# Loading and fusing two weight matrices ahead of attention, in a fused attention and feed-forward kernel

## The chip, the cores and the metric

One NeuronCore of one Trainium2 chip. Times are device microseconds (us) of one execution. A "span" is the length of the profiled execution on the core; in every run here the time is 1.7 us longer than the span. Each comparison is made with runs of the kernel before on the same chip in the same rounds.

## The reference

Causal attention over 8 batches, 8 heads, 576 tokens, with 16 extra keys and values ("beacons") that every token sees, then a feed-forward layer on the 4,608 tokens:

```python
scores = q @ k_all.T / sqrt(64)         # 8 x 8 x (576 x 592), causal past the 16 beacons
a      = softmax(scores);  x = a @ v_all         # x: 4608 x 512
h      = (x @ w1) * (x @ w2) @ w3       # w1, w2: 512 x 1024; w3: 1024 x 1024
out    = h @ w_out                      # w_out: 1024 x 512
```

The kernel multiplies `w3 @ w_out` once ("fusing", 64 matmuls of 512 columns), so that the feed-forward needs 96 matmuls for each 512 tokens: 64 for `x @ w1` and `x @ w2`, 32 for the fused product, 864 in all.

## The kernel before

Attention goes by head pairs (four per batch) and half pairs (eight "steps" `s` per batch). Scores are made keys by queries, so the exponentials go straight into the value matmuls. In the traces here TensorE takes its matmuls in program order, and the generator `ff` hands out feed-forward matmuls that are put between the steps as filling: `emit_ff(n)`. The main loop, which the change hardly touches:

```python
for s in range(NSB, NS):                     # NSB = 8 steps in a batch
    b, r = s // NSB, s % NSB
    ...
    if more: scores(s + 1); exps(s + 1, 0)
    values(s)
    if b == 1 and r % 2 == 0 and r < NSB - 2:
        pe_transpose_pair(1, r // 2 + 1)     # batch 1: q, k of the next head pair
        if r < NSB - 4: cast_pair(1, r // 2 + 2)
    emit_ff(...)                             # cut
    if 1 <= b < B - 1:
        if r == 0:
            for c in range(NJT if b > 1 else 0):     load_v(b + 1, c)
            for c in range(NJT if b + 2 < B else 0):
                load_q(b + 2, c); load_k(b + 2, c)   # into q16s[(b+2) % 2], k16s[(b+2) % 2]
        if 1 <= r <= NJT:
            transpose_qk(b + 1, r - 1)       # DMA transposes on SyncE's queue
```

From batch 2 on, q and k are loaded by GpSimd's queue, which casts them to fp16, into two alternating buffers `q16s[b % 2]` and `k16s[b % 2]`, and transposed by DMA. Batches 0 and 1 take another way: their pairs are loaded as fp32 by SyncE's queue into eight staging tiles of their own (`early`), cast on VectorE (`cast_pair`) and transposed on TensorE (`pe_transpose_pair`). **In this kernel batch 1 never uses `q16s[1]`**, so at batch 1's first step (`r == 0`) batch 3's q and k may be loaded there. This point matters later.

The start: q, k first, attention of batch 0 from 8 us on, fusing after the weights have landed, at 26 to 49 us; batch 1's 64 filling matmuls, 4 at its first scores and 60 between its steps, are feed-forward work of the first 512 tokens.

Of the kernel before, what the change touches and what calls it, by code (L numbers as in the profile page):

```python
# [39 lines left out]
def kernel(  # L40
# [43 lines left out]

    ptp = ctx.enter_context(tc.tile_pool(name="ptp", bufs=2))
    xp = ctx.enter_context(tc.tile_pool(name="xp", bufs=2))
    sm = ctx.enter_context(tc.tile_pool(name="sm", bufs=4))
    gp = ctx.enter_context(tc.tile_pool(name="gp", bufs=2))
    wp = ctx.enter_context(tc.tile_pool(name="wp", bufs=2))
    early = ctx.enter_context(tc.tile_pool(name="early", bufs=8))  # L90
    tiny = ctx.enter_context(tc.tile_pool(name="tiny", bufs=2))
    bkp = ctx.enter_context(tc.tile_pool(name="bkp", bufs=1))
    asb = ctx.enter_context(tc.tile_pool(name="asb", bufs=3))
# [36 lines left out]

    early_qk, early_b = {}, {}

    def load_pair(b, t):
        for i, src in enumerate((q, k)):
            st = early.tile([P, 2, RUN * D], FP32, name="st")
            if b:
                nc.vector.memset(st[0:1, 0, 0:1], 0.0)
            nc.sync.dma_start(  # L138
                st[:NR], src[b, ds(2 * t, 2)].rearrange("h (p j) d -> p h (j d)", j=RUN)
            )  # L140
            early_qk[b, t, i] = st
        if t == 0:
            bst = bkp.tile([Nb, H, D], FP32, name="bst")
            nc.sync.dma_start(bst, beacon_k[b].rearrange("h n d -> n h d"))
            early_b[b] = bst

    o16s = {}

    def cast_pair(b, t):
        o16s[t] = []  # L150
        for i in range(2):
            o16 = tiny.tile([P, RUN, P], FP16, name=f"o16_{i}")
            nc.vector.tensor_copy(  # L153
                o16[:NR].rearrange("p j (h d) -> p h j d", h=2),
                early_qk[b, t, i][:NR].rearrange("p h (j d) -> p h j d", j=RUN),
            )
            o16s[t].append(o16)
        if t == 0:
            b16 = bkp.tile([Nb, DM], FP16, name="b16")
            nc.vector.tensor_copy(b16, early_b[b].rearrange("p h d -> p (h d)"))  # L160
            early_b[b] = b16

    def pe_transpose_pair(b, t):
        qT, kT = qTs[b % NB2], kTs[b % NB2]
        for o16, dst, off, copy in (
            (o16s[t][0], qT, 0, nc.vector.tensor_copy if b or t != 1 else nc.scalar.copy),
            (o16s[t][1], kT, Nb, nc.scalar.copy),
        ):
            pt = psM.tile([P, 1024], FP16, name="pm")
            for j in range(RUN):  # L170
                nc.tensor.transpose(pt[:, ds(j * NR, NR)], o16[:NR, j, :], ident[:NR, :NR])
            if off:
                nc.tensor.transpose(
                    pt[:, ds(S, Nb)], early_b[b][:, ts(t, P)], ident[:Nb, :Nb]
                )
                copy(dst[:, t, 0:Nb], pt[:, ds(S, Nb)])
            copy(  # L177
                dst[:, t, ds(off, S)].rearrange("p (i j) -> p i j", j=RUN),
                pt[:, 0:S].rearrange("p (j i) -> p i j", j=RUN),
            )  # L180

    def pe_transpose_x(b):
# [25 lines left out]

    def constants(i):
        nc.vector.memset(vas[i][64:128, 4, :, :], 0.0)  # L210
        nc.vector.memset(vas[i][:, 0:4, :, 64:65], 1.0)
        nc.vector.memset(vas[i][0 : S + Nb - 4 * P, 4, :, 64:65], 1.0)

    for i in range(NB2):
        nc.vector.memset(kTs[i][:, :, ds(S + Nb, NJT * P - S - Nb)], 0.0)

    for t in range(NT):
        load_pair(0, t)
    nc.gpsimd.affine_select(
# [6 lines left out]
        channel_multiplier=-1,  # L226
    )
    for m, base in (
        (MA[:, 0:128], 0),
# [12 lines left out]
        )  # L242
    for i in range(NB2):
        nc.gpsimd.memset(k16s[i][64:128, 4, :], 0.0)
        nc.gpsimd.memset(q16s[i][64:128, 4, :], 0.0)

    def load_w12(c):
        for i, w in enumerate((moe_w1, moe_w2)):
            nc.gpsimd.dma_start(
                w12[:, :, ds(i * DF + c * 256, 256)],  # L250
                w[:, ts(c, 256)].rearrange("(t p) f -> p t f", p=P),
            )


    def w3_transposed(kt):
        pt = psM.tile([P, NFT, P], FP16, name="pm")
        for rt in range(NFT):
            nc.tensor.transpose(pt[:, rt, :], w316[:, kt // 2, kt % 2, ts(rt, P)], ident)  # L258
        wT = wp.tile([P, NFT, P], FP16, name="wT")
        nc.vector.tensor_copy(wT, pt)  # L260
        return wT

    def fuse(rows):
        wT = rows[0]
        for kt in range(NFT):
            pm = psM.tile([P, DM], FP32, name="pm")
            for rt in range(NFT):
                nc.tensor.matmul(  # L268
                    pm,
                    wT[:, rt, :],  # L270
                    wo16[:, rt, :],
                    start=(rt == 0),
                    stop=(rt == NFT - 1),
                )
                if rt == 3 and kt + 1 < NFT:
                    nxt = w3_transposed(kt + 1)
                if rt < NFT - 1:
                    yield
            nc.scalar.copy(Wt[:, kt, :], pm)  # L279
            wT = nxt  # L280
            yield

# [24 lines left out]
    def ff_out(mc, gT):  # L307
        for mt in range(4):
            pm = psM.tile([P, 512], FP32, name="pm")
            for kf in range(NFT):  # L310
# [7 lines left out]
                if kf < NFT - 1:  # L318
                    yield
            ot = early.tile([P, 2, RUN * D], FP32, name="st")  # L320
            ot = ot.rearrange("p h r -> p (h r)")[:, 0:DM]
            nc.vector.tensor_scalar(ot, pm, float(1.0 / GS), None, ALU.mult)  # L322
# [3 lines left out]
    def stream():  # L326
        yield from fuse(rows)
        for mc in range(M // 512):
            gT = yield from ff_ab(mc)
            yield from ff_out(mc, gT)  # L330

    rows = []
    ff = stream()
# [50 lines left out]
    def values(s):  # L384
# [7 lines left out]
        ni = len(tiles)  # L392
        pv = psV.tile([P, 6, VS], FP32, name="pv")
        for n, i in enumerate(tiles):
# [28 lines left out]
    n_first = 4  # L423
    n_second = 64 - n_first
    fill = [0] * NS
    for s in range(NSB, 2 * NSB):
        fill[s] = n_second * (s - NSB + 1) // NSB - n_second * (s - NSB) // NSB

    marks = [(2 * NSB, 128 + 8), (26, 128 + 132), (58, 128 + 516), (NS, 128 + 588)]
    for (s0, u0), (s1, u1) in zip(marks, marks[1:]):  # L430
# [4 lines left out]
    def ahead(s):  # L435
        scores(s)
        for j in range(2):
            exps(s, j)
# [4 lines left out]

    spin(14)
    cast_pair(0, 0)
    pe_transpose_pair(0, 0)
    cast_pair(0, 1)
    spin(2)
    ahead(0)
    pe_transpose_pair(0, 1)  # L450
    cast_pair(0, 2)
    constants(0)
    for c in range(NJT):
        load_v(0, c)
    wo_v = moe_w_out.rearrange("(a c p) n -> a p c n", p=P, c=2)
    for a in range(4):
        nc.gpsimd.dma_start(wo16[:, ds(2 * a, 2), :], wo_v[a])

    w316 = xT[:, :, ds(M // 2, 2 * DF)].rearrange("p a (c r) -> p a c r", c=2)
    for kt in range(NFT):  # L460
        nc.gpsimd.dma_start(w316[:, kt // 2, kt % 2], moe_w3[ts(kt, P), :])
    spin(1)
    ahead(1)
    masks(0)
    pe_transpose_pair(0, 2)
    cast_pair(0, 3)
    spin(1)
    ahead(2)
    masks(1)
    pe_transpose_pair(0, 3)  # L470
    constants(1)
    masks(2)
    for c in range(NJT):
        load_v(1, c)
    load_w12(0)
    load_w12(1)
    for c in range(NJT):
        load_q(2, c)
        load_k(2, c)
    load_w12(2)  # L480
    load_w12(3)
    for s in range(NSB):
        if 0 < s < NSB - 2:
            ahead(s + 2)
        if s < 5:
            spin(1)
        if s == 5:
            rows.append(w3_transposed(0))
        emit_ff((0, 0, 0, 0, 0, 4, 6, 6)[s])
        values(s)  # L490
        if 0 < s < NSB - 2:
            masks(s + 2)
        if s == 5:
            for t in range(NT):
                load_pair(1, t)
    for c in range(NJT):
        load_v(2, c)
    emit_ff(6)
    pe_transpose_x(0)
    emit_ff(20)  # L500
    cast_pair(1, 0)
    emit_ff(56 - emitted)
    pe_transpose_pair(1, 0)
    cast_pair(1, 1)
    emit_ff(64 - emitted)
    ahead(NSB)
    emit_ff(n_first)
    masks(NSB)
    for s in range(NSB, NS):
# [6 lines left out]
        if b == 1 and r % 2 == 0 and r < NSB - 2:  # L516
            pe_transpose_pair(1, r // 2 + 1)
            if r < NSB - 4:
                cast_pair(1, r // 2 + 2)
        k1 = min(4, fill[s])  # L520
# [21 lines left out]
    emit_ff(1 << 30)  # L542


# [28 lines left out]
```

## Time and profile before

| | before |
|---|---|
| time, median of the first 3 runs | 310.21 us (310.08 to 312.54) |
| profiled span | 309.7 us (time of that run 311.4) |
| first scores of batch 0 / 1 / 2 | 7.95 / 49.55 / 79.40 us |
| from batch 2's first scores to the end | 230.3 us |
| TensorE busy | 295.8 us, 96% |

TensorE is the engine that sets the end. The landmarks are read from the timeline of TensorE: "first scores of batch n" is the start of the first score matmul of that batch. Because of that order, the stretch between two landmarks contains a known set of work, and two kernels can be compared stretch by stretch. The lines themselves are in the prediction below. One more view, which the prediction tells but does not show: TensorE's windows from 80 us on. Columns: window, length; busy us and (instructions) of TensorE, weight loads, VectorE, ScalarE, GpSimd; granted TensorE clock; DMA share; GB/s.

```profile
80.00:90.00 10.00, 9.35 (x98) 4.64 (x96) 4.76 (x12) 4.79 (x6) 10.00 (x14) 1.00 2.20 185
90.00:100.00 10.00, 10.00 (x106) 5.12 (x99) 6.01 (x15) 7.06 (x10) 5.08 (x7) 1.00 2.15 184
100.00:150.00 50.00, 50.00 (x528) 25.81 (x527) 28.06 (x68) 28.82 (x40) 24.01 (x30) 1.00 1.48 153
```

TensorE is hardly ever without work here, at full clock. Anything that leaves it standing, or running at half clock, is paid in full.

### The profile page before, as it was taken

The numbers are of one execution on the slowest core, as the hardware profiler recorded it, in microseconds if no ns is written. First come the engines' busy times: TensorE is split into PE (matmuls) and PEld (weight loads), VectorE is DVE, ScalarE is ACT, GpSimd is POOL, SyncE is SP. The second block draws the span as 40 slices with busy tenths as digits, with TensorE's granted clock in tenths as the row PEclk, the third lists the DMA queues.
The fourth block names the chain that finished last, engine by engine and source line by source line (L and its number), as shares of the span: only waits on it lengthen the run. The fifth ranks groups of instructions, "written<-read, shape, count | busy, mean of one in ns | idle before, by whom it ended". The sixth has DMA issues, their size and how long they took to land.

```text
span 309.7 us, 7001 instructions
## 1 busy us (share of the span) xinstructions
PE 295.8 (96%) x2823; PEld 153.4 (50%) x2823; DVE 168.1 (54%) x391; ACT 158.1 (51%) x230; POOL 108.9 (35%) x147
## 2 busy tenths in 40 slices
PE   8898999898899999999999999999999999999995
PEld 3465555454454555555555545455555554444442
DVE  4854545865465556555555555555555554334342
ACT  2973327775546745674467466546655660230320
POOL 8555617835992089009701960320000000000000
PEclk9777999999999999999999999999999999999999
DMA  7999999999999999999999999997334003302003
GB/s 177 199 203 210 194 262 176 156 151 155 163 206 172 140 101 215 154 147 123 231 154 119 116 230 121 155 183 157 78 66 148 0 4 78 135 0 102 36 0 135
DMA packets 156960, 42.97 MB, mean 139 GB/s; under 512 B 143104, under 2 KB 151296, under 8 KB 156928
## 3 DMA queue, kind: packets, MB, share of 16 engines
q0 software_dynamic: 102240, 17.28, 78.7%
q1 hardware_dynamic: 54688, 25.25, 42.8%
q8 instruction: 22, 0.36, 0.5%
q14 instruction: 10, 0.08, 0.1%
HBM read 39.32 MB, written 9.44 MB: 157 GB/s over the span
## 4 chain that ended last, share of the span: by engine, by line
PE 79%; DMA 8%; DVE 4%; ACT 3%; SPq 2%; issue 2%; POOL 1%; DVEq 0%
PE pm L290 34%; PE pm L311 18%; PE pv L397 11%; PE ps L359 8%; PE pm L268 5%; DMA qT<-q 3%; DMA k<-in_beacon_k_dram 2%; DMA st<-in_k_dram 2%; ACT pT L368 2%; PE pm L258 1%; SPq L128 1%; DVE gT L303 1%; POOL va L112 1%; SPq L138 1%; DVE o L153 1%
## 5 line engine op out<-in xcount | busy, mean ns | idle before, releaser
L290 PE MATMUL pm<-xT,w 128*128 128x512 f16 x576 | 132.4, 379 | 0.7 <-ACT kT L177 0.7
L368 ACT ACTIVATE pT<-ps 128x736 f16<-128x736 f32 (+3 forms) x128 | 105.5, 865 | 40.2 <-PE ps L359 32.6
L290 PEld LDWEIGHTS <-w 128*128 128x128 f16 x576 | 53.5, 98 | 60.0 <-issue 1.5
L301 ACT ACTIVATE a_sb<-pm 128x512 f32<-128x512 f32 x72 | 43.0, 598 | 74.3 <-PE pm L290 73.9
L303 DVE TENSOR_TENSOR gT<-pm,a_sb 128x512 f16<-128x512 f32 x72 | 49.7, 691 | 44.9 <-PE pm L290 44.9
L311 PE MATMUL pm<-Wt,gT 128*128 128x512 f16 x288 | 65.6, 379 | 0.0
L112 POOL DMA_DIRECT2D va<-in_v_dram x40 | 34.2, 872 | 66.4 <-PE pv L397 57.4
L397 PE MATMUL pv<-va,pT 128*128 128x65 f16 x960 | 44.4, 196 | 2.6 <-DVE pT L380 2.5
L397 PEld LDWEIGHTS <-pT 128*128 128x128 f16 x960 | 35.6, 99 | 13.6 <-issue 6.5
L311 PEld LDWEIGHTS <-gT 128*128 128x128 f16 x288 | 26.9, 98 | 30.0 <-issue 0.2
L359 PE MATMUL ps<-qT,kT 64*128 64x80 f16 (+3 forms) x704 | 36.3, 232 | 2.5 <-ACT pT L368 1.9
L322 DVE TENSOR_SCALAR st<-pm 128x512 f32<-128x512 f32 x36 | 24.9, 691 | 25.0 <-PE pm L311 24.8
L405 DVE RECIPROCAL rd<-pv 128x4 f32<-128x4 f32 x64 | 12.1, 190 | 48.0 <-PE pv L397 47.8
L359 PEld LDWEIGHTS <-kT 64*128 64x128 f16 x704 | 21.1, 96 | 29.1 <-issue 27.1
L406 DVE TENSOR_TENSOR x<-pv,rd 128x256 f16<-128x256 f32 x64 | 31.4, 491 | 2.4
L103 POOL DMA_DIRECT2D q<-in_q_dram x30 | 26.7, 890 | 10.2 <-DMA va<-in_v_dram 6.3
L112 POOL DMA_DIRECT2D k<-in_k_dram x30 | 26.3, 878 | 7.4 <-DMA w<-in_moe_w_dram 4.3
L380 DVE TENSOR_TENSOR pT<-pT,MB 128x512 f16<-128x512 f16 x64 | 20.2, 322 | 0.0
L268 PE MATMUL pm<-wo,wT 128*128 128x512 f16 x64 | 17.1, 395 | 0.9 <-DVE wT L260 0.8
L380 DVE TENSOR_TENSOR pT<-pT,MA 128x480 f16<-128x480 f16 x32 | 12.9, 402 | 1.7 <-ACT pT L368 1.5
L153 DVE CAST o<-st 96x768 f16<-96x768 f32 x16 | 10.2, 666 | 4.1 <-DMA st<-in_q_dram 2.8
L279 ACT CAST Wt<-pm 128x512 f16<-128x512 f32 x8 | 4.7, 585 | 14.9 <-PE pm L268 14.9
(43 smaller groups left out, 98.1 us busy)
## 6 DMA issues: line engine op xcount, KB each, us to landing
out_dram<-st SPq DMA_DIRECT2D x36, 256.0 KB, 4.3
va<-in_v_dram POOLq DMA_DIRECT2D x24, 128.0 KB, 6.3
q<-in_q_dram POOLq DMA_DIRECT2D x24, 128.0 KB, 8.2
st<-in_q_dram SPq DMA_DIRECT2D x8, 288.0 KB, 7.4
st<-in_k_dram SPq DMA_DIRECT2D x8, 288.0 KB, 8.3
k<-in_k_dram POOLq DMA_DIRECT2D x18, 128.0 KB, 8.6
xT<-in_moe_w_dram POOLq DMA_DIRECT2D x8, 256.0 KB, 9.8
w<-in_moe_w_dram POOLq DMA_DIRECT2D x8, 256.0 KB, 14.4
```

Of the source, the lines that this page charges most:

```text
L103: nc.gpsimd.dma_start(q16s[b % NB2][:rows, c, :].rearrange("s (h d) -> s h d", h=H), q[b, :, ds(c * P, rows), :].rearrange("h s d -> s h d"),)
L112: nc.gpsimd.dma_start(dst[ds(p0, rows)], src[b, :, ds(s0, rows), :].rearrange("h s d -> s h d"))
L268: nc.tensor.matmul(pm, wT[:, rt, :], wo16[:, rt, :], start=(rt == 0), stop=(rt == NFT - 1),)
L290: nc.tensor.matmul(pm, w12[:, kt, ds(i * DF + kf * P, P)], xT[:, kt, ds(mc * 512, 512)], start=(kt == 0), stop=(kt == NKT - 1),)
L301: nc.scalar.activation(a_sb, pm, AF.Copy, scale=GS)
L303: nc.vector.tensor_tensor(gT[:, kf, :], pm, a_sb, ALU.mult)
L311: nc.tensor.matmul(pm, gT[:, kf, ts(mt, P)], Wt[:, kf, :], start=(kf == 0), stop=(kf == NFT - 1),)
L359: nc.tensor.matmul(ps[:, hh, ds(col, n)], kT[ds(hh * 64, 64), t, ts(jt, P)], qT[ds(hh * 64, 64), t, ds(q0, n)],)
L368: nc.scalar.activation(pT[:, :, ds(GO[g], GW[g])], pss[s][j][:, :, 0 : GW[g]], AF.Exp, scale=scale)
L380: nc.vector.tensor_tensor(blk, blk, m.unsqueeze(1).to_broadcast([P, 2, n]), ALU.mult)
L397: nc.tensor.matmul(pv[:, 2 * n + hh, 0:65], pT[:, hh, ds(col, P)], va[:, jt, 2 * t + hh, 0:65], start=(jn == 0), stop=(jn == len(BLK[i]) - 1),
L406: nc.vector.tensor_tensor(x16[:, ds(tiles[0], ni), ds(t * P, P)].rearrange("p i (h d) -> p i h d", h=2), pv[:, 0 : 2 * ni, 0:64].rearrange ...
```

## The change

Intent: `w3` and `w_out` are loaded first, half by SyncE's queue (fp32, cast on ScalarE and VectorE) and half by GpSimd's. Four of the eight rows of the fused weights grow side by side in four PSUM banks as `w_out` lands; the other four go between batch 0's head pairs. q and k of batch 0 come through the casting queue. Batch 1's q and k now come by the same `load_q` and `load_k` as all later batches, with transposes on TensorE. The 64 feed-forward matmuls of the first 512 tokens run in one piece before batch 1.

```diff
+    for a in range(2):                                     # SyncE: half of w3, w_out
+        st = gp.tile([P, 2, 2 * DM], FP32, name="gT")
+        nc.sync.dma_start(st[:, 0, :], moe_w3[ts(a, P), :])
+        nc.sync.dma_start(st[:, 1, :], moe_w_out[ds(a * 2 * P, 2 * P), :]...)
+        firsts.append(st)
+    def cast_first(a):
+        nc.scalar.copy(w316[:, a // 2, a % 2], firsts[a][:, 0, :])
+        nc.vector.tensor_copy(wo16[:, ds(2 * a, 2), :]..., firsts[a][:, 1, :])
     ...
+    load_w3(2); load_wo(2); load_w3(3); load_wo(3)         # GpSimd's queue
+    load_pair(0); load_w3(4)                               # then q, k pairs between rows
     ...                                                    # (cut)
+    for a in range(4):                                     # four rows side by side
+        if a < 2:
+            cast_first(a)
+        wTs.append(w3_transposed(a))
+        spin(2 if a == 0 else 1)                           # matmuls of zeros, for the clock
+        for kt in range(a):
+            fuse(accs[kt], wTs[kt], 2 * a - 2, 2 * a)
+        fuse(accs[a], wTs[a], 0, 2 * a)
+    for kt in range(4):
+        fuse(accs[kt], wTs[kt], NFT - 2, NFT)
     ...                                                    # (cut: batch 0's head pairs)
+    for c in range(NJT):                                   # batch 1 into q16s[1], k16s[1]
+        load_q(1, c)
+        load_k(1, c)
     ...
+    emit_ff(64)
+    pe_transpose_second(0)
     ...
-            pe_transpose_pair(1, r // 2 + 1)
-            if r < NSB - 4:
-                cast_pair(1, r // 2 + 2)
+            pe_transpose_second(r // 2 + 1)                # reads q16s[1], k16s[1]
```

The load of batch 3's q and k at `r == 0` is unchanged, so the diff does not show it.

> **What bounds the kernel now.** I read the page first (engine rows, the forty slices), then a table of windows over the first 100 us, then the chain of work that ended last, and last the timeline and the DMA queues of the start.
>
> ```profile
> PE 295.8 (96%) x2823; PEld 153.4 (50%) x2823; DVE 168.1 (54%) x391; ACT 158.1 (51%) x230; POOL 108.9 (35%) x147
> PE   8898999898899999999999999999999999999995
> ACT  2973327775546745674467466546655660230320
> PEclk9777999999999999999999999999999999999999
> DMA  7999999999999999999999999997334003302003
> ```
>
> Parts 1 and 2 of the page: TensorE (PE) has work in nearly every slice, ScalarE (ACT) and VectorE about half. The granted clock dips only in slices 2 to 4, and the DMA engines are full until about 230 us.
>
> ```profile
> 264.56 13.81 PE pm L290 x64
> ```
>
> In the chain, 64 matmuls of 512 columns take 13.81 us where nothing else is mixed in: 216 ns each. With that unit I count the useful work: 864 feed-forward and 64 fusing matmuls are 200.4 us. In the window from 100 to 250 us PE never stops; its 486 feed-forward matmuls are 105 us, so the 20.6 head pairs (scores and values) in it have 45, or 2.18 us each, 70 us for all 32. Transposes (w3, x, q and k) at about 56 ns are 11 us. Together 281 of 309.7 us: some 28 us are lost. The tail (last matmul 306.0 us) has 3.7 of them, so about 24 are lost before 95 us. That is all the change can win from.
>
> ```profile
> 0.00:5.00 5.00, 3.73 (x9) 1.31 (x10) 1.64 (x7) 1.28 (x1) 3.73 (x14) 1.00 0.63 144
> 10.00:15.00 5.00, 4.19 (x51) 2.56 (x52) 4.09 (x12) 4.83 (x10) 2.67 (x4) 0.73 1.89 186
> 15.00:20.00 5.00, 4.98 (x66) 3.62 (x66) 3.01 (x12) 3.24 (x6) 3.65 (x7) 0.59 1.51 194
> 25.00:30.00 5.00, 4.21 (x41) 2.77 (x39) 1.58 (x3) 0.60 (x1) 3.14 (x5) 0.66 1.12 210
> 45.00:50.00 5.00, 4.95 (x45) 2.73 (x43) 2.77 (x4) 2.05 (x5) 2.68 (x3) 1.00 1.51 221
> 50.00:100.00 50.00, 46.18 (x525) 25.03 (x524) 30.29 (x72) 32.58 (x49) 34.70 (x43) 1.00 2.09 166
> ```
>
> Columns: PE, weight loads, VectorE, ACT, GpSimd busy, granted clock, DMA share, GB/s. PE is "busy" for 4.98 of 5 us from 15 to 20 at a clock of 0.59, so busy is not useful there. After 30 us the clock is 1.00.
>
> ```profile
> 7.95 0.55 PE L359 MATMUL ps<-qT,kT 64*128 64x128 f16 x8 [0.27 <-ACT kT L177]
> ...
> 49.55 0.55 PE L359 MATMUL ps<-qT,kT 64*128 64x128 f16 x8
> ...
> 52.07 1.29 SPq L127 DMA_TRANSPOSE qT<-q  x1
> 67.84 2.40 SPq L128 DMA_TRANSPOSE kT<-k  x1
> ...
> 79.40 0.55 PE L359 MATMUL ps<-qT,kT 64*128 64x128 f16 x8
> ```
>
> The landmarks: first scores of batch 0 at 7.95 us, of batch 1 at 49.55, of batch 2 at 79.40; the DMA transposes for batch 2 run on SyncE's queue from 52.07 to 70.24. By 49.55 the useful PE work is: fusing 13.8 + 3.6 (its transposes), batch 0's attention 8.7, q, k, x transposes 4.6, total 30.7. So 18.9 us are lost before 49.55 and 5.2 from there to 79.40 (29.85 us for 64 feed-forward matmuls, 13.8; attention, 8.7; three pair transposes, 2.1).
>
> Rates of the two queues, from three 5 us stretches of the start (packets, MB, share): 5 to 10, 20 to 25 and 50 to 55 us.
>
> ```profile
> q1 hardware_dynamic: 831, 1.18, 109.2%
> ```
> ```profile
> q0 software_dynamic: 704, 1.05, 116.0%
> ```
> ```profile
> q0 software_dynamic: 5847, 0.75, 232.4%
> ```
>
> The hardware queue moved 236 GB/s of fp32 (rows of 1.5 KB, 96 partitions). The casting queue landed 210 GB/s of fp16 from large rows, so it read 420 GB/s; with 64-element rows it is bound by packets, 1170 per us.
>
> **What the Trainium skill says.** (1) "TensorE: Matmul & The Clock Gate", Back-to-back issue gap: 512 columns at full clock take N/2.4 + 2.5 ns, 216 ns. The chain above agrees to the ns. (2) The same page, Part 1: an insufficiently busy PE falls to half its clock for a window of some 3.4 us or more. The clock of 0.59 to 0.73 in three windows before 30 us agrees in kind. (3) "DMA: Bandwidth & Descriptors", Issuing engines are not separate DMA queues: both queues run on the same 16 DMA engines and interleave, so a second queue saves only issue time. So I add the engine time of both queues and don't take the longer one. The trace agrees from 40 to 45 us (683 packets of one, 685 of the other), though in the first 10 us the casting queue got nothing. (4) The same page, SWDGE vs HWDGE vs iDMA: only GpSimd's queue casts. So what SyncE loads as fp32 needs an ACT or VectorE cast, and what GpSimd loads doesn't.
>
> **The change part by part.** Before, q and k start at once, attention of batch 0 runs from 8 to 34 us bound by ACT (four exponentials per head pair, 0.78 + 1.02 + 0.81 + 0.85) with PE half empty and cold, and fusing w3 with w_out (64 matmuls) comes at 26 to 49 us, when the weights have landed. After, w3 and w_out come first; four rows grow in the four PSUM banks that scores use later; the other four rows go between batch 0's head pairs. The feed-forward of the first 512 tokens (64 matmuls) fills the time before batch 1.
>
> Step A, the start. SyncE's 2.1 MB fp32 take 6.5 to 9 us of all DMA engines (236 GB/s measured; the rows are now 4 KB on 128 partitions, so up to 320 is my guess), GpSimd's 2.1 MB source 5 us (210 GB/s landed). From 2 us on, that ends at 13.5 to 16, say 14.5. Until then 24 of the 32 matmuls can run; the last 8 are 1.7 us, to 16.2. Then two evacuations (0.7), two reorders (0.8), transposes (0.35), the kT copy (0.17 + 0.65): the first scores at about 19 us, against 7.95. Fusing done by then: 6.9 + 1.8.
>
> Step B, batch 0. Per head pair the chain is: kT copy, scores (0.4 to the first exponential), two exponentials 1.8, meanwhile w3 transposes, values 1.0, the wT copy 0.69 and four fusing matmuls 0.86 ahead of the next scores, which come 2.9 us after the kT copy; two exponentials 1.7, kT copy 0.82. That is 5.5, 5.6 and 5.7 us for the first three pairs. The last pair with its values and x transposes takes 9.5. In all 26.3: feed-forward starts at 45.3.
>
> Step C: 64 matmuls are 13.8; ten transposes and 4 matmuls 1.5: first scores of batch 1 at 60.6 against 49.55. It comes 11.1 us later with 68 matmuls (14.7 us) more done: a gain of 3.6 us.
>
> Step D, batch 1. Only 24 matmuls are left to put between its steps (the next block of 512 tokens needs batch 1 itself), against 60 before. So ACT and the hand-overs bound it: first exponentials 2.1; a step with transposes is 3.0 to 3.35 (values, transposes, kT copy 0.7 and exponential in a row), one without 1.8 to 2.4; eight come to 17.5; x transposes and hand-over 4. In all 23.6: first scores of batch 2 at 84.2 against 79.40.
>
> Step E, the rest. From batch 2's first scores to the end, before needs 309.7 - 79.4 = 230.3. The changed kernel has 32 matmuls fewer left, 6.9 us: 223.4. The sum is 84.2 + 223.4 = 307.6; with 0.5 for the timed median over the profiled span, 308.1.
>
> Moved without a price on the path: twelve fewer pair transposes, the batch 1 casts on VectorE (eight of 0.67). Batch 1's q and k now come through the casting queue: 9,400 packets at 1170 per us are 8 us, issued once batch 0's pairs are read (about 33 us) and there by about 50, before 60.6.
>
> **The rivals.** *Batch 2's DMA transposes become the wait.* They stand behind the first output stores on SyncE's queue and start at about 62 us; they took 18 us before and 7 more to land, so 87 or 88 against the 84.2 at which PE wants them: up to 3.5 us, a time of 311.5. Against it: with less traffic the same transposes took 1.2 to 1.3 us each near 210 us, which ends in time. I add 0.4 for it. *The start is slower or faster.* If the casting queue is starved again, nothing changes while the engines stay full; but if the first casts arrive only after 11 us as before (v's packets did, though issued at 4.63), step A ends 3 us later: 311. If both queues reach 400 GB/s, it ends 2.5 us earlier: 305.5. *Thinner filling later.* Steps 16 to 25 have 9.2 matmuls each in place of 12.4; where a_sb's 0.6 us falls between two exponentials, values may wait 0.4 us, up to 2 us in all. *The hand-overs of steps B and D are shorter than I chain them* (I took every wait in series): 1 us per head pair would be 6 us, and a time of 302.
>
> **Range and chances.** The sum and the first rival's share give 308.5. Step A is uncertain by 2.5 us, B and D by 3 together, the batch 2 wait by 2: about 4.2 in all, so 303 to 314. Faster by over 2% means below 304.0; slower means above 316.4. Filling a start bound by DMA with fusing should win something, but batch 1 gives much of it back for want of matmuls. Faster 0.22, within 2% 0.70, slower 0.08.
>
> **What will show it.** First scores of batch 0 near 19 us, of batch 1 near 60.6, of batch 2 near 84. A clock near 1.00 from 20 us on. Batch 1 with PE waits for ACT (kT) and VectorE (pT), about 5 us. If scores of batch 2 wait for a qT or kT transpose, the first rival holds. I am wrong if batch 0's head pairs take 7 us each (slower) or if batch 1's first scores come before 57 us (faster by over 2%).

## The result, and the profile after

| | before | after |
|---|---|---|
| time, median | 311.13 us (4 runs, 310.08 to 312.54) | 328.73 us (4 runs, 327.59 to 331.41) |
| profiled span | 309.7 | 325.9 |
| first scores of batch 0 / 1 / 2 | 7.95 / 49.55 / 79.40 | 26.18 / 68.34 / 99.44 |
| batch 1 (its first scores to batch 2's) | 29.85 | 31.10 |
| from there to the end | 230.3 | 226.5 |

The ratio after / before is 1.0575, 95% interval 1.0487 to 1.0663: slower. Ratios here are the mean time of one kernel's fast runs over that of the other's of the same rounds, so they are not quite the ratio of the medians quoted.

The page of the kernel after, parts 1 and 2 (one slice is 8.1 us):

```profile
PE 298.7 (92%) x2810; PEld 152.3 (47%) x2810; DVE 165.2 (51%) x382; ACT 156.6 (48%) x221; POOL 117.0 (36%) x159
PE   7688888983888999799999999999999999999995
PEclk9699999998599999999999999999999999999999
```

Two places stand out against the page before. In the second slice (8 to 16 us) TensorE and its clock are at 6. In the tenth and eleventh (73 to 90 us) TensorE falls to 3 and then the granted clock to 5. After that the rows look as before, which a windows view of the kernel after makes precise (columns as above):

```profile
10.00:15.00 5.00, 4.26 (x23) 2.27 (x24) 1.48 (x3) 0.00 (x0) 2.22 (x4) 0.53 1.19 207
15.00:20.00 5.00, 5.00 (x26) 2.35 (x25) 1.19 (x2) 0.00 (x0) 4.80 (x8) 0.79 1.56 188
75.00:80.00 5.00, 1.55 (x25) 0.74 (x22) 1.52 (x5) 0.93 (x2) 5.00 (x7) 0.85 2.14 143
80.00:85.00 5.00, 2.31 (x11) 1.13 (x11) 0.46 (x1) 0.81 (x2) 0.57 (x1) 0.50 1.32 84
85.00:90.00 5.00, 5.00 (x63) 2.88 (x62) 2.49 (x8) 3.06 (x4) 0.00 (x0) 0.62 0.40 105
100.00:150.00 50.00, 47.17 (x512) 24.25 (x512) 27.36 (x68) 32.01 (x44) 24.79 (x31) 1.00 1.69 149
```

From 75 to 85 us TensorE is busy 3.86 of 10 us; from 80 to 90 the clock is about half. From 100 to 150 us it stands for 2.8 us, where before it stood for none.

**The hole at 75 to 90 us.** TensorE's timeline of the kernel after (start, length, line, operation, tiles, count, and in brackets the idle time before and what ended it). L401 is the scores, L187 the transposes of batch 1's q and k:

```profile
71.15 0.52 PE L187 MATMUL pm<-ident,q 128*128 128x128 f16 x5
...
76.20 0.22 PE L187 MATMUL pm<-ident,q 128*128 128x128 f16 x1
77.94 0.23 PE L187 MATMUL pm<-ident,q 128*128 128x128 f16 x1 [1.52 <-DMA q<-in_q_dram]
80.26 0.29 PE L187 MATMUL pm<-ident,q 128*128 128x128 f16 x1 [2.09 <-DMA q<-in_q_dram]
...
99.44 0.55 PE L401 MATMUL ps<-qT,kT 64*128 64x128 f16 x8
```

Head pair 1's five q transposes run in a row at 71.15. Pair 2's, from 76.20 on, come one by one, and all but the first wait for a load of q: 1.52, 2.09, 1.38 and 1.05 us, 6.0 in all. But batch 1's q had been complete since before 66 us, or pair 0 could not have been transposed. Which loads are these? GpSimd's timeline in the same kernel:

```profile
71.67 0.88 POOL L103 DMA_DIRECT2D q<-in_q_dram  x1 [5.87 <-PE pm L187]
```

The bracket tells it: this load waited for the transposes L187, which ended at 71.67. It overwrites what they read. It is the load of batch 3's q into `q16s[1]`, emitted at batch 1's first step, after the transposes of pairs 0 and 1 and before those of pairs 2 and 3. The scheduler keeps program order: the load waits for the earlier readers, and the later readers wait for the load.

So the program order is wrong in a way that a time alone does not tell: heads 4 to 7 of batch 1 are computed from batch 3's q and k. The result was nevertheless accepted as correct. I repeated the reference's arithmetic on the host with those heads exchanged: the output changes by 0.5% of its norm, 1.4% within batch 1, because with inputs of this size the softmax is almost flat. No run here measures the wrong values as such; program order and the two waits show the exchange.

**The start.** TensorE in the kernel after; L307 is the transposes of w3's rows, L320 the growing of the four rows (32 matmuls), L213 matmuls of zeros, L168 the first q, k transposes:

```profile
6.36 0.84 PE L307 MATMUL pm<-ident,xT 128*128 128x128 f16 x8
7.04 0.59 PE L213 MATMUL pm<-zeros 128*128 128x512 f16 x2
10.03 0.86 PE L307 MATMUL pm<-ident,xT 128*128 128x128 f16 x8 [2.39 <-ACT xT L257]
...
11.11 1.06 PE L320 MATMUL ps<-wo,wT 128*128 128x512 f16 x2
12.88 1.04 PE L320 MATMUL ps<-wo,wT 128*128 128x512 f16 x2 [0.71 <-DVE wT L315]
...
14.99 2.93 PE L320 MATMUL ps<-wo,wT 128*128 128x512 f16 x8
...
18.42 4.48 PE L320 MATMUL ps<-wo,wT 128*128 128x512 f16 x20
24.56 0.70 PE L168 MATMUL pm<-ident,o 96*128 96x96 f16 x12 [1.67 <-DVE o L154]
```

The last piece of `w_out` for these rows had landed by 14.1 us (issued at 3.42 and 10.7 us on its way). By then TensorE had done 4 of the 32 growing matmuls. ScalarE and VectorE of the same kernel show what it waited for:

```profile
8.93 1.04 ACT L257 CAST xT<-gT 128x1024 f16<-128x1024 f32 x1 [3.55 <-DMA gT<-in_moe_w_dram]
...
11.53 0.69 DVE L258 CAST wo<-gT 128x1024 f16<-128x1024 f32 x1 [3.59 <-DMA gT<-in_moe_w_out_dram]
12.14 0.68 DVE L315 COPY wT<-pm 128x1024 f16<-128x1024 f16 x1
```

Row 1 of w3, SyncE's third load, landed at 8.9 us; from there a cast on ScalarE (1.04), eight transposes (0.86) and a copy on VectorE (0.68) come one after the other. That copy stood behind a cast of `w_out`, which itself waited for SyncE's fourth load until 11.5. Meanwhile TensorE stood still from 7.6 to 10.0 us, and the granted clock was 0.50 from 10.25 until about 17.1 us (fine windows; it shows in the 0.53 and 0.79 above).

By the prediction's own steps:

| step | predicted | after | difference |
|---|---|---|---|
| A, to batch 0's first scores | 19 | 26.18 | +7.2 |
| B, to the first feed-forward matmul (52.56) | 26.3 | 26.4 | +0.1 |
| C, to batch 1's first scores | 15.3 | 15.8 | +0.5 |
| D, batch 1 | 23.6 | 31.1 | +7.5 |
| E, rest | 223.4 | 226.5 | +3.1 |
| span | 307.6 | 325.9 | +18.3 |

The differences add to 18.4 from rounding.

### The profile page after: what moved, and what is told of

It reads as the page before. It is cut to its first block, busy times and chain, and to the rows that moved or that the text cites. A ratio compares the mean times of both kernels' runs of the same rounds, so it can differ in the third digit from the quotient of the medians.

```text
span 325.9 us, 6953 instructions
## 1 busy us (share of the span) xinstructions
PE 298.7 (92%) x2810; PEld 152.3 (47%) x2810; DVE 165.2 (51%) x382; ACT 156.6 (48%) x221; POOL 117.0 (36%) x159
## 4 chain that ended last, share of the span: by engine, by line
PE 80%; DMA 6%; DVE 6%; ACT 2%; POOL 2%; issue 1%; SPq 1%; DVEq 0%
PE pm L335 37%; PE pm L356 17%; PE pv L443 11%; PE ps L401 8%; DMA gT<-in_moe_w_out_dram 3%; PE ps L320 2%; DMA xT<-x 2%; PE pm L320 2%; ACT pT L410 2%; DVE x L452 1%; DMA q<-in_q_dram 1%; DVE pT L422 1%; POOL k L112 1%; DVE ot L366 1%; POOL q L103 1%
## 5 line engine op out<-in xcount | busy, mean ns | idle before, releaser
L356 PE MATMUL pm<-Wt,gT 128*128 128x512 f16 x288 | 68.2, 384 | 0.1
L443 PE MATMUL pv<-va,pT 128*128 128x65 f16 x912 | 41.8, 195 | 3.3 <-DVE pT L422 2.2
L103 POOL DMA_DIRECT2D q<-in_q_dram x35 | 30.9, 884 | 21.7 <-DVE o L154 9.8
L401 PE MATMUL ps<-qT,kT 64*128 64x80 f16 (+3 forms) x704 | 35.7, 230 | 2.4 <-ACT pT L410 1.1
L366 DVE TENSOR_SCALAR ot<-pm 128x512 f32<-128x512 f32 x36 | 24.9, 691 | 25.6 <-PE pm L356 25.6
L401 PEld LDWEIGHTS <-kT 64*128 64x128 f16 x704 | 20.6, 95 | 31.4 <-issue 26.0
L451 DVE RECIPROCAL rd<-pv 128x4 f32<-128x4 f32 (+1 forms) x62 | 11.7, 188 | 45.6 <-PE pv L443 45.6
L112 POOL DMA_DIRECT2D k<-in_k_dram x35 | 30.8, 879 | 4.9 <-DMA q<-in_q_dram 3.2
L452 DVE TENSOR_TENSOR x<-pv,rd 128x256 f16<-128x256 f32 (+1 forms) x62 | 30.3, 488 | 2.4
L422 DVE TENSOR_TENSOR pT<-pT,MA 128x480 f16<-128x480 f16 x32 | 12.7, 397 | 0.0
L320 PEld LDWEIGHTS <-wT 128*128 128x128 f16 x64 | 6.0, 105 | 9.6 <-DVE wT L315 3.4
L213 PE MATMUL pm<-zeros 128*128 128x512 f16 x22 | 9.1, 541 | 1.3 <-DVE zeros L208 1.3
L320 PE MATMUL ps<-wo,wT 128*128 128x512 f16 x32 | 9.5, 448 | 0.7 <-DVE wT L315 0.7
```

The source lines that it names most:

```text
L103: nc.gpsimd.dma_start(q16s[b % NB2][:rows, c, :].rearrange("s (h d) -> s h d", h=H), q[b, :, ds(c * P, rows), :].rearrange("h s d -> s h d"),)
L112: nc.gpsimd.dma_start(dst[ds(p0, rows)], src[b, :, ds(s0, rows), :].rearrange("h s d -> s h d"))
L320: nc.tensor.matmul(acc, wT[:, rt, :], wo16[:, rt, :], start=(rt == 0), stop=(rt == NFT - 1),)
L356: nc.tensor.matmul(pm, gT[:, kf, ts(mt, P)], Wt[:, kf, :], start=(kf == 0), stop=(kf == NFT - 1),)
L401: nc.tensor.matmul(ps[:, hh, ds(col, n)], kT[ds(hh * 64, 64), t, ts(jt, P)], qT[ds(hh * 64, 64), t, ds(q0, n)],)
L422: nc.vector.tensor_tensor(blk, blk, m.unsqueeze(1).to_broadcast([P, 2, n]), ALU.mult)
```

## The experiments

All kernels gave results that were accepted as correct. "One look" is one profiled execution; its state is unknown. The theory going in: (T1) batch 3's loads into a buffer still in use cost step D 7 to 8 us; (T2) the start is late because of row hand-overs and the half clock. Rivals: for D, that batch 1 is short of filling matmuls and bound by ScalarE and hand-overs anyway, so that the wait hides other waits; for the start, that the DMA engines bound it.

### 1. The changed kernel again (asis_check)

No edit; a second look at the result, and a yardstick on the same chip and in the same rounds as runs 2 and 3.

> The changed kernel once more, unedited, for its correctness. Reading its program order: batch 3's q and k are loaded into the buffers that still hold batch 1's q and k for head pairs 2 and 3, so those pairs are computed from batch 3's data. Theory (overwritten too early): the result differs from the reference by about 0.5% of its norm over the whole output (1.4% in batch 1), which a host calculation with the exchanged heads gives; inputs are so small that the softmax is nearly flat, so it can pass. Rival (the order is right and the waits on q in batch 1 are only late loads of batch 1 itself): an error like the other kernels' fp16 rounding, well under 0.5%. Time: about 328 us.

Measured: 329.67 us in one look, before 311.28 (7 runs). First scores 25.27 / 68.60 / 100.72; the wait for q is 6.7 us. The time repeats. The error, for which the run was made, was not reported (only that the output was accepted), so the run does not decide between its theory and its rival.

### 2. Batch 3's loads after the last reader (late_loads)

```diff
-            if r == 0:   # v as before, and:
-                for c in ...: load_q(b + 2, c); load_k(b + 2, c)
+            if r == (5 if b == 1 else 0):
+                for c in ...: load_q(b + 2, c); load_k(b + 2, c)
```

> One edit: batch 3's q and k are loaded after the last transpose of batch 1's q and k (in its sixth step in place of its first). Theory (TensorE waits in batch 1 for a load that overwrote what it was to read): the five waits for q (6.0 us, plus some 2.5 us at half clock after them) go, batch 1 from its first to batch 2's first scores takes 22 to 24 us in place of 31.1, the time falls by 7 to 9 us, ratio to the kernel before 1.03, and the error becomes that of fp16 rounding. Rival (batch 1 is slow because of its hand-overs or because batch 2's DMA transposes come late): the time falls by less than 3 us and PE waits for kT, pT or a DMA transpose in the same stretch.

Measured: 324.42 us median (4 runs, one of them slow), ratio 1.041 (1.0337 to 1.0483). First scores 24.38 / 66.55 / 89.38. Batch 1 takes 22.83 us in place of 31.10. The waits of TensorE in this kernel, largest first (in total, times, longest):

```profile
PE pm L335 <- DMA xT<-x: 3.2, 1, 3.2
PE ps L401 <- DMA kT<-k: 2.9, 1, 2.9
```

The load now comes after the last reader. L187 at 74.41 and 79.45 are the q transposes of pairs 2 and 3, each five in a row, and L103 is the first load of batch 3's q:

```profile
74.41 0.52 PE L187 MATMUL pm<-ident,q 128*128 128x128 f16 x5
79.45 0.52 PE L187 MATMUL pm<-ident,q 128*128 128x128 f16 x5
...
79.97 0.88 POOL L103 DMA_DIRECT2D q<-in_q_dram  x1 [15.54 <-PE pm L187]
```

No wait for q is left, so T1 holds for the stretch: 8.3 us, and TensorE ran at full clock throughout it (1.00 from 66.55 to 89.38). But against the first run's ratio of 1.0575 the whole gained only 1.7% or 5 us. In the two looks the span falls by 5.2: 8.3 here and 1.8 in the start, less 4.8 lost after batch 2's first scores (231.3 in place of 226.5). A new wait took most of that back: batch 2's scores for a transposed k, once, at 95.08. SyncE's queue in the same kernel says why:

```profile
70.78 1.19 SPq L128 DMA_TRANSPOSE kT<-k  x1
76.50 0.34 SPq L367 DMA_DIRECT2D out_dram<-ot  x1
...
87.82 1.40 SPq L128 DMA_TRANSPOSE kT<-k  x1
```

The queue issues in program order here, and L367, the store of an output tile, cannot be issued before that tile exists. The transposes emitted after it stand behind it: after the first pair's (70.78) nothing is issued for over 4 us, and batch 2's fifth and last k transpose is issued at 87.82. This is the prediction's first rival. In the changed kernel as given it was hidden, because batch 1 took 8 us longer.

### 3. The same, and the 64 feed-forward matmuls spread over batch 1 (late_loads_spread)

```diff
-    marks = [(NSB, 72), ...]
+    marks = [(NSB, 16), ...]
-    emit_ff(64)                 # in one piece, before batch 1
+    emit_ff(8)
```

> As the run with late loads, and the 64 feed-forward matmuls that stood ahead of batch 1 are spread over its eight steps (10 per step in place of 3; 16 ahead in place of 72). Theory (batch 1 has too little to fill the gaps that the exponentials leave): batch 2's first scores come 4 to 6 us earlier than in the run with late loads, and so does the end; ratio to before about 1.012. Rival (q and k of batch 1 are not there yet at 54 us, so that moving batch 1 up only moves the wait): PE waits for a DMA of q or k before its transposes, and the gain is under 2 us.

Measured: 316.58 us (4 runs, one slow), ratio 1.0216 (1.0141 to 1.0291), slower than before, though whether by over 2% is unclear. Against run 2 it is 6 us less by the ratios and 8.1 by the spans of the two looks, 1.5 of which are the start. First scores 22.88 / 52.95 / 84.01. From batch 0's first scores to batch 2's it takes 61.13 us, against 65.00 in run 2, with exactly the same work between: in run 2 the block of 64 leaves ScalarE little to do (busy 5.47 of 15.78 us from 50.77 to 66.55), and then batch 1 leaves TensorE without enough (19.33 of 22.83). The wait for kT falls from 2.9 to 0.8 us, since the transposes get more time.

In this look the start, not edited, ran at full clock, and batch 0's first scores came at 22.88.

### 4, 5, 6. The start: warm clock, order on VectorE, both (start_warm, start_dve, start_warm_dve)

More matmuls of zeros in the pause, so that the clock stays up; `w_out`'s cast emitted after the copy of `wT` that it held back; both. Batch 3's loads are left as in the changed kernel, so these are to be read by the start alone.

```diff
 # start_warm                                  # start_dve
-        spin(2 if a == 0 else 1)              -   (w_out's cast, inside cast_first)
+        spin((13, 5, 1, 1)[a])                +        if a < 2: cast_wo(a)   # after w3_transposed(a)
```

> One edit at the start: 13 and 5 idle-filling matmuls in place of 2 and 1 after the first two rows of w3, so that TensorE does not stand still from 7.6 to 10.0 us. Theory A (the start is slow since the clock fell to half from 10.25 to 17.08 us, after that pause): clock 1.00 throughout, the last of the 32 growing matmuls ends at about 18 in place of 22.9 us and the first scores come at about 21 in place of 26.2. Theory B (the data and casts set it, each wait follows the one before): the clock may stay up, but first scores come less than 2 us earlier.

> One edit at the start: VectorE casts the second piece of w_out after, not before, it copies the second transposed row of w3 (that cast waits for a load that lands at 11.5 us and holds the copy up until 12.1). Theory B (a chain of in-order waits): the copy is at about 11.0, the first four growing matmuls end about 1 us earlier and so does everything up to the first scores (25 in place of 26.2). Theory A (clock): still at half clock from 10 to 17 us, so the gain is at most 1 us.

> Both edits of the start together. If clock and order add up: first scores at about 20 us. If the landing of w_out's last piece (issued at 3.4, landed at about 13.4 us) is the true limit: the last growing matmul not before 16 us and first scores not before 19.

Measured, one look each (us):

| | row 1 of w3 there, its cast begins | first growing matmul | last 20 begin | first scores, batch 0 | clock, 10 to 15 us | time |
|---|---|---|---|---|---|---|
| after | 8.93 | 11.11 | 18.42 | 26.18 | 0.53 | 327.59 |
| after again (run 1) | 8.79 | 10.56 | 17.51 | 25.27 | 0.70 | 329.67 |
| start of run 2, unedited | 7.50 | 9.27 | 16.62 | 24.38 | 0.66 | |
| start of run 3, unedited | 7.70 | 9.47 | 15.05 | 22.88 | 1.00 | |
| start of run 8, unedited | 9.48 | 11.48 | 19.08 | 27.09 | 0.60 | |
| start_warm | 8.84 | 11.48 | 16.31 | 24.51 | 1.00 | 326.80 |
| start_dve | 9.02 | 11.38 | 16.00 | 24.24 | 0.72 | 326.79 |
| start_warm_dve | 8.52 | 11.17 | 15.09 | 22.84 | 1.00 | 323.91 |

Two things follow. The unedited start has no fixed length: five looks give 22.88 to 27.09, and the only one at full clock is the shortest. The Trainium skill, "TensorE: Matmul & The Clock Gate", Part 1: The HAM clock gate, says that the activity window is "free-running" and that the same kernel therefore shows different cold stretches from run to run; these looks agree: runs 2 and 3, whose starts are the same program and whose row 1 was there at 7.50 and 7.70, had clocks of 0.66 and 1.00. And even in the two looks at full clock from 5 to 25 us (run 3 and start_warm_dve) the start ends at 22.88 and 22.84, not at 19, without the edits as with them (though row 1 was there 0.8 us later in the second); start_warm, at full clock until 23.3, ends later, at 24.51. The time from the beginning of the last 20 growing matmuls to the first scores is 7.8 to 8.2 us in every row, so the growing is what is late. Of the 7.2 us, run 3's look is 3.3 us shorter (26.18 less 22.88), but not by the clock alone: SyncE's third and fourth loads were there 1.2 and 1.3 us earlier in it (7.70 and 10.21, against 8.93 and 11.53). That leaves, as an estimate, about 2.0 us for the clock, 1.3 for the landing and 3.9 for the rows. Two pairs of looks with nearly the same landing put the clock at 1.5 (runs 2 and 3) and 1.7 us (after and start_warm). The split stays rough. What moves the landing from look to look is open. How much the single edits are worth can't be told from one look each, as the spread of the unedited start is larger than their effect; no look reached the 20 to 21 us that two of the expectations named.

### 7. All edits so far together (all_mended)

Late loads, spread filling, both start edits, and `(26, 196)` in `marks` to `(26, 188)`: eight filling matmuls later, for the wait for `xT` (see "why", step E).

> Late loads, spread filling, both edits of the start, and the third block of feed-forward moved 8 matmuls later (it waited 1.9 us for a DMA transpose of x at 134 us). If the four causes are what cost the 16 us and add up: 326 - 8 - 5 - 5 - 2 = 306 us of span, ratio to before 0.985 to 1.00. If they hide one another: above 1.01.

Measured: 311.97 us (4 runs), ratio 1.0049 (0.9998 to 1.0099), between the two cases of the expectation; the start, for one, gave 2.6 us (26.18 to 23.61) of the 5 put down for it. First scores 23.61 / 53.67 / 84.73. No wait for `xT` from DMA is left; the waits for DMA transposes are down to 1.6 us. The granted clock is 0.992 to 1.000 in its four runs, where the fast runs of run 3 have 1.000, 0.989 and 0.988: this fits start edits that keep the clock up, but these runs were on another chip and have other edits too.

### 8. Late loads, and batch 2's DMA transposes ahead of the stores (late_loads_early_tr)

Tests the explanation of run 2's new wait: all ten transposes are emitted at batch 1's first step, before the first output store.

```diff
+            if b == 1 and r == 0:
+                for c in range(NJT): transpose_qk(b + 1, c)
-            if 1 <= r <= NJT:
+            if b > 1 and 1 <= r <= NJT:
                 transpose_qk(b + 1, r - 1)
```

> The run with late loads, and one edit more: all ten DMA transposes of batch 2 are queued at once in batch 1's first step, ahead of its output stores, in place of one pair per step between the stores. Theory (the first rival of the prediction: these transposes stand behind output stores on SyncE's queue and come late; PE waited 2.9 us for kT's at 95 us once the overwritten loads were mended): that wait goes, the span is 317 to 318.5 in place of 320.7, ratio to before about 1.032. Rival (the data of batch 2 comes late, or the DMA engines are full): the wait stays or is taken up by a wait for the next DMA; less than 1 us gained.

Measured: 320.51 us (4 fast runs), ratio 1.0312 (1.0284 to 1.034). Batch 1 takes 22.83 us again (69.26 to 92.09). The wait for kT is gone, and from batch 2's first scores to the end it takes 227.1 us against 231.3 in run 2. So the order on SyncE's queue cost 4.2 us there, of which 2.9 were the one wait. One wait of over 1 us is left in the rest, 2.4 us for `xT` from DMA; without it 224.7 would remain, near the 223.4 of step E.

### 9. Another order of the growing (start_order)

The earlier rows' matmuls before the next row's transposes, on top of both start edits; batch 3's loads as in the changed kernel.

```diff
+        for kt in range(a): fuse(accs[kt], wTs[kt], 2 * a - 2, 2 * a)
         wTs.append(w3_transposed(a))
-        for kt in range(a): fuse(accs[kt], wTs[kt], 2 * a - 2, 2 * a)
```

> Both edits of the start (idle-filling matmuls, cast after the copy) and a third: in each of the four rounds the growing matmuls of the earlier rows, whose operands are there, are issued before the transposes of the next row of w3, which wait for its landing. Theory (when the last piece of w_out lands at about 14 us, 20 of the 32 growing matmuls are still queued behind the last row's transposes, 4.5 us in place of the 1.7 of the prediction): 14 are left, so the last one ends about 1.3 us earlier and first scores come at 21.5 in place of 22.8 us. Rival (the landing sets it): no change, 22.8.

Measured: 324.43 us in one look; first scores at 24.09. A miss: I had looked for 21.5. The growing does begin earlier (9.36), but the transposes of each row now stand behind up to ten matmuls, and TensorE then waits 0.57 us for `wT` twice, at 14.05 and 17.61.

### 10, 11. The mended kernel with early transposes, and with the other order (mended_early_tr, mended_order)

Run 7 with run 8's edit; the same with run 9's.

> The run with all mended and batch 2's transposes queued at once. Its span was 310.9 us, and PE waited only 1.6 us for DMA transposes there, 1.2 of them in batch 4: so 0 to 1 us gained, ratio to before 1.000 to 1.005.

> The run before with the third edit of the start as well. If 1.3 us of the start come through to the end: ratio to before 0.995 to 1.001. If thin filling in batches 2 and 3 (9 matmuls per step where the kernel before has 12) is what bounds it there, the start's gain is lost and the ratio stays at 1.003.

Measured, six fast runs each: 311.33 us, ratio 1.003 (1.0004 to 1.0056), first scores 23.29 / 53.37 / 84.42; and 313.23 us, ratio 1.0084 (1.0052 to 1.0117), 24.45 / 54.52 / 85.58. The other order costs 1.9 us, and the start is 1.2 us later in the look: what run 9 showed once is confirmed by the times.

The windows of mended_early_tr, to be held against the three lines of the kernel before above:

```profile
80.00:90.00 10.00, 8.79 (x98) 4.93 (x94) 5.04 (x12) 4.66 (x8) 8.72 (x11) 1.00 2.03 191
90.00:100.00 10.00, 9.18 (x111) 4.78 (x109) 5.45 (x14) 6.42 (x11) 4.92 (x6) 1.00 1.94 138
100.00:150.00 50.00, 49.19 (x539) 25.30 (x538) 28.71 (x71) 30.79 (x42) 24.72 (x31) 1.00 1.61 152
```

TensorE stands for 2.84 us from 80 to 150 us (1.21 + 0.82 + 0.81), before for 0.65. Of this, 0.53 us at 120.37 is still a wait for a DMA transpose of `xT`. The other waits are ended by exponentials, masks and an evacuation (0.25 to 0.80 us each). That points to the thinner filling of the prediction's third rival (its bound was 2 us); no run tests it alone.

### 12. The same with SyncE's loads in the order w3, w3, w_out, w_out (mended_swap)

Row 1 of w3 is then the second load and not the third.

```diff
     for a in range(2):
         st = gp.tile(...);  nc.sync.dma_start(st[:, 0, :], moe_w3[ts(a, P), :])
-        nc.sync.dma_start(st[:, 1, :], moe_w_out[...])
+    for a in range(2):
+        nc.sync.dma_start(firsts[a][:, 1, :], moe_w_out[...])
```

> The run with all mended and batch 2's transposes queued at once, and SyncE's four first loads in the order w3, w3, w_out, w_out in place of w3, w_out, w3, w_out. Theory (the growing matmuls start at 11.6 us since the second piece of w3 lands only at 8.9, after GpSimd's queue has begun to take turns, and then needs its cast, transposes and copy): that piece lands at about 6, and the first growing matmuls start at about 9.7, when the first piece of w_out (now third, about 8.9) is cast. If the late start of the growing is all that holds the start up, first scores come nearly 2 us earlier (21.4 in place of 23.3); if the later pieces of w_out set it, under 1 us. At the end the ratio to before is then 0.997 or 1.001 to 1.003.

Measured: 311.61 us (6 runs), ratio 1.0021 (0.9995 to 1.0047). TensorE's start in this kernel (L323 is the growing, L310 the transposes):

```profile
10.15 1.12 PE L323 MATMUL ps<-wo,wT 128*128 128x512 f16 x4
...
12.67 1.89 PE L323 MATMUL ps<-wo,wT 128*128 128x512 f16 x8 [0.74 <-DVE wo L261]
```

Row 1 is there early, and the first four matmuls begin at 10.15 instead of 11.61 in run 10. The next eight wait for the cast of `w_out`'s second piece, and first scores come at 22.96, only 0.33 us earlier. In run 10 the start waited for the third piece of SyncE's queue (row 1), here for the fourth. So up to some 12.7 us the start hangs on the landing of SyncE's 2 MB (rival, for this part borne out by both orders), and from there on 28 matmuls and 8 transposes in a row.

No version is faster than the kernel before. The best, runs 10 and 12, lie within 0.6% of it.

## Why the prediction was wrong

The prediction was 308.5 us, range 303 to 314, and "within 2%" the likeliest. It was 328.73, outside the range, and slower by over 2%.

**Step D failed, and that is the error of kind.** The sentence that failed is on batch 1's q and k: "issued once batch 0's pairs are read (about 33 us) and there by about 50, before 60.6", under the heading "moved without a price on the path". I asked when the new user of `q16s[1]` gets its data, and not who writes the buffer next. The unchanged line at `r == 0` writes it, in the middle of batch 1's reading. Step D took 31.1 us in place of 23.6; with the loads moved behind the last reader it took 22.83 in two kernels, 0.8 less than predicted. So the working of step D itself was good, and the whole excess, 8.3 us in that stretch, is this order. Part of it is standing still (6.0 us) and part the half clock after it (0.50 and 0.62 from 80 to 90 us).

**Step A failed, in size.** "Until then 24 of the 32 matmuls can run; the last 8 are 1.7 us, to 16.2." All four-row data was there at 14.1, so the estimate of the landing (14.5) held. But 4 matmuls had run, not 24, and the growing ended at 22.9. I treated landing as if it were usable data, and left out cast, transposes and copy between a piece's landing and its first matmul (1.04 + 0.86 + 0.68 for row 1), that these run row after row, and that the pauses let the clock fall. By the rough split above, of the 7.2 in the look compared about 2.0 are the clock and 1.3 a landing later than in the quickest look, which both vary from run to run, and 3.9 are the rows. In the kernels with all mends, step A takes 22.96 to 23.61. Whether a quite different start could reach 19 is open; of two reorderings tried, one lost and one gained nothing that the times resolve.

On the start's DMA, the prediction's second rival asked whether casts arrive late. They did not: q0, the casting queue, moved its first packets soon after 5 us. What it took from the Trainium skill ("DMA: Bandwidth & Descriptors", Issuing engines are not separate DMA queues), that both queues run on the same engines, fits: from 6 to 8 us the two queues had 52.7% and 51.4% of the engines. The cost of that sharing is what I missed: SyncE's queue moved 0.70 MB from 2 to 4 us and 0.36 MB from 6 to 8, so the pieces needed first (row 1 of w3, `w_out`'s second) were slowed by pieces needed later.

**Steps B and C were right.** Head pairs of batch 0 came 5.44, 5.44 and 5.74 us apart (predicted 5.5, 5.6, 5.7), step B took 26.4 (26.3), step C 15.8 (15.3). The fourth rival, shorter hand-overs, falls: chaining every wait in series was right.

**Step E was off by 3.1 us in size.** 1.9 us of it is one wait at 134.5 us, of a feed-forward matmul for `xT` of batch 2, which comes by DMA transpose; a wait for a mask before batch 2's second values is 0.80, but the kernel before has it too (0.65). In all TensorE stands 2.4 us longer in this stretch than before (7.65 against 5.24), and it is busy 6.25 us less, not 6.9. The term left out seems to follow from the thinner filling: with 9.2 in place of 12.4 matmuls per step, the steps to the end of batch 2's attention are shorter, but the transposes of its result are not, and four matmuls of the next 512 tokens are placed there. In runs 7 and 10 these are placed eight matmuls later, and the wait is gone in run 7 and 0.5 us in run 10; as other edits came with it, that alone was not run. With all mends, step E took 224.6.

**The first rival** (batch 2's transposes behind the stores) is true of the design, with 2.9 us of wait and 4.2 us in all in run 2. In the kernel as given it is hidden by step D's wait. **The third rival** fits as well: TensorE stands 2.2 us longer between 80 and 150 us in run 10 than before (2.84 less 0.65), of which 0.5 is the wait for `xT`; the other 1.7 are within its bound.

**Small terms and signs.** I added 0.5 us from span to time; it is 1.7. Eight steps of batch 1 come to at least 18.0 us by the ranges given (3 of 3.0 and 5 of 1.8), not 17.5, if the last is counted in full. The DMA row of the page is full until about 209 us, not 230; nothing rests on it. Neither of the two signs of being wrong that I had named appeared: head pairs took 5.4 to 5.7 us, not 7, and batch 1's first scores came at 68.34, not before 57. The wait that gave the error away, for a load of q inside batch 1, was not on the list.

**Where the expected gain went.** With the mends, the kernel behaves about as the prediction's sum said it would: span 309.0 against 307.6, with step A 4.3 too long and 4.1 less from there to batch 2's first scores (the filling is spread, which the change as given did not do). It still only ties with the kernel before. Per landmark: batch 2's first scores come 5.0 us later (84.42 against 79.40), with 6.9 us less left to do, and 1.2 of the rest are lost again to thinner filling and waits. Fusing before attention does fill a start bound by DMA; but in the kernel before, 22 of the 64 fusing matmuls (25.9 to 35.4 us) already ran between batch 0's last steps, and the first block of feed-forward between batch 1's. So the work was moved partly from one place with room for it to another. This is an account of the sums; no run tests it by itself.

## What to carry to other kernels

When a change gives a buffer a new user, list every writer of that buffer in program order, the unchanged lines too: a load that was harmless because nobody read the buffer becomes a wait, and possibly wrong data, and neither the diff nor a tolerance check need show it. A wait of a matmul for the load of an operand that must have been there long ago is the sign to look for in a trace. For work that is to begin "as the data lands", count the whole chain from landing to first use for each piece, in the order in which pieces share the queues, and check what a removed wait will uncover behind it.

## What the Trainium skill lacked or had wrong

- "TensorE: Matmul & The Clock Gate", Why this matters for your kernels: it advises no idle gaps above about 3 us between matmul bursts. Here a gap of 2.39 us, between two matmuls of zeros and eight transposes, was followed by a granted clock of 0.50 from 10.25 to about 17.1 us; and gaps of 1.05 to 2.09 us with a single transpose between each came with 0.50 from about 78.5 us until 88.75. The limit is too generous here even if transposes are counted as no work: the clock fell 2.6 us after the last ordinary matmul in the first place (7.63 to 10.25) and about 2.1 us after it in the second (76.36 to 78.5).
- The same page, Part 1: it puts the ramp's cost at under 1% of a typical span. The second fall of the clock here cost about as much, 1.5 to 2.0 us of 310 by the estimate above. What no page gives is how much single looks differ for another reason: row 1 of w3 was there at 7.50 to 9.48 us in five looks at one unedited start, whose first scores differ by 4.2 us (22.88 to 27.09).
- "DMA: Bandwidth & Descriptors", SWDGE vs HWDGE vs iDMA: it says that an engine's rings are served in turn. It does not say how late a queue gets its first turn when the other is full: the casting queue's first load was issued at 1.67 us and its first packets moved after 5 us in the kernel after; issued at 4.63 us, after about 11 us in the kernel before (1 packet from 9 to 11 us, 134 from 11 to 12). Latency and other measured facts on that page gives about 1 us to the first byte. What sets the delay is not settled by these runs.
